# Moving matmul operands to 160 bytes modulo 256 in a two-layer linear-attention and MLP kernel

## The chip, the core and the metric

The kernel runs on one core of a Trainium2 chip. The core has a matmul engine (TensorE, PE in the profile; its weight loads are listed apart as PEld), a vector engine (VectorE, DVE), a scalar engine for activations (ScalarE, ACT), a general engine (GpSimd, POOL) and an engine that here only issues transfers (SyncE, SP). They work on an on-chip memory of 128 partitions; matmul results land in PSUM, in banks of 512 floats a partition. A matmul reads two operands from on-chip memory: the stationary one, which a weight load puts into the array beforehand, and the moving one, which is then streamed through it. "128x448 moving" means 128 partitions by 448 columns.

The metric is the device time of one launch in microseconds (us). Addresses in this document are byte offsets within a partition; a float takes 4 bytes.

## The reference

Input `x` has 2048 tokens of 448 features. Two identical layers follow each other:

```python
def _A_ref(x, wqkv, wo):                       # linear attention, 16 heads of 28
    q, k, v = split(x @ wqkv)
    phi = lambda t: where(t > 0, t + 1, exp(t)) + 1e-6
    pq, pk = phi(q), phi(k)
    kv = einsum("bhsd,bhse->bhde", pk, v)
    z = einsum("bhsd->bhd", pk)
    num = einsum("bhqd,bhde->bhqe", pq, kv)
    den = einsum("bhqd,bhd->bhq", pq, z)[..., None] + 1e-6
    return merge_heads(num / den) @ wo
def _B_ref(x, w1, b1, w2, b2):                 # MLP, 448 -> 1792 -> 448
    return gelu(x @ w1 + b1) @ w2 + b2

x = x + _A_ref(_layernorm(x), wqkv, wo)
x = x + _B_ref(_layernorm(x), w1, b1, w2, b2)  # and both once more
```

## The kernel before

Every large product is computed from split operands. A float32 value `a` becomes `hi` (rounded to the matmul's reduced format, float32r in the code) and `lo = a - hi`, and a product takes three matmuls: hi by hi, hi by lo, lo by hi. A contraction over 448 features is cut into three chunks of 128 and one of 64. The last 64 hold hi and lo stacked in one 128-row operand, so they take two matmuls. One product of 128 tokens therefore takes 3 x 3 + 2 = 11 matmuls.

A layer runs in these stages.

1. `phase1` goes over 16 tiles of 128 tokens. Per tile: normalized tokens are transposed and split into blocks `XH` and `XL`. `proj` (lines 328 to 333) multiplies them, as stationary operands, by the moving pieces of wk or wq (`wkq`), into `psk` and `psq`. `phi` is applied; the keys are split into `kh` (`stage_kh`, line 464) and `kl`. The untransposed normalized tokens are split into `xnh` and `xnl` (`stage_s`). `stage_g` (lines 526 to 541) accumulates G = tokens-transposed by keys: stationary `xnh` or `xnl`, moving `kh` or `kl`. A projection and a G group alternate on TensorE. The queries of some tiles are projected only later, as filling between the steps of stage 2. Queries go to memory as `pq_d`.
2. A transition turns G into one matrix per group of heads with wo folded in, M, split into `Mh` and `Ml` (`trans_ms`). M is copied by transfers into the places of wq, in chunks of 128 rows (`trans_chunks`), since wq is not needed any more.
3. The attention output of four tiles at a time: `o_mm` (lines 792 to 794, first block, moving `Mh`, `Ml`) or `oc_mm` (lines 803 to 807, later blocks, moving the chunks in wq's places), with stationary `qh` and `ql`.
4. The MLP, in four blocks of 512 tokens by 14 slices of 128 hidden features: `mlp1` (lines 861 to 865) has the weights stationary and 512 tokens moving, `hp`. Gelu gives `gh` and `gl`. `mlp2` (lines 894 to 896) has these stationary and `w2h`, `w2l` moving, 448 columns, `y`. The attention output of the next block (`oc_mm`) is worked in between slices after a plan (`PLAN_0`, `PLAN_1`, `PLAN`).

The order of instructions on every engine is written out by hand (`ORDER`, `STEPS`, `LAUNCH`, the plans), and nothing is rescheduled. Engines meet only at semaphores. Transfers are issued on SP's queue in the same written order.

Where tiles lie matters here. Tiles are named by tags; a tag has a fixed number of buffers, placed one behind another where the tag is first used. `t448` makes tiles of 448 floats, 1792 bytes, which is 7 x 256. `t512` makes tiles of 512 floats, or of 576 floats for tags B and F, of which a slice of 512 from column `at` is used. Both sizes are multiples of 256 bytes, and two small tiles named `space` fill up so that the operands of matmuls start on multiples of 256. Three kinds of tile are set off from that by `APART = 28` floats, 112 bytes: `xnl` and `gl` and `ql` of `q_split` (tag B), and `ql` of `q_part` (tag F). These are the lo parts that serve as stationary operands in G, in the second MLP product and in the attention output. All other operands of these matmuls lie at 0 modulo 256.

The pieces of wk have tags W0, W1, W2 (hi of chunks 0 to 2), W3, W4, W5 (lo) and W6 (the stacked last chunk); those of wq have V0 to V6 likewise (`piece`, line 132). W0 to W3 later hold loaded queries (`load_pq`), W4 and W5 products of them, W6 the masked G product `kvm`. V0 to V2 and V6 later hold M's hi chunks and its stacked chunk, V3 to V5 the lo chunks.

Of the kernel before, what the change touches and what calls it, by code (L numbers as in the profile page):

```python
# [9 lines left out]
F32 = mybir.dt.float32  # L10
F32R = mybir.dt.float32r
# [11 lines left out]
def linear_attn_mlp_kernel(  # L23
# [15 lines left out]
    S, D = x0.shape  # L39
    F = w1.shape[1]  # L40
# [4 lines left out]
    G = 112  # L45
# [6 lines left out]
    work = ctx.enter_context(tc.tile_pool(name="work", bufs=2))  # L52
# [14 lines left out]
    def t448(tag, bufs, name, dt=F32):  # L67
        bufs = NH if tag == "H" else bufs
        return work.tile([128, D], dt, name=name, tag=tag, bufs=bufs)

    APART = 28

    def t512(tag, bufs, name, dt=F32, at=0):
        n = 576 if tag in "BF" else 512
        return work.tile([128, n], dt, name=name, tag=tag, bufs=bufs)[:, at:at + 512]

    def f(ap):
        return ap.bitcast(F32)
# [53 lines left out]
    def piece(name, i):  # L132
        return t448(f"{'W' if name == 'k' else 'V'}{i}", 1, f"w{name}{i}", F32R)

    def split_hi(name, c, st):
        hi = piece(name, c if c < 3 else 6)
        act.copy(hi, st[c])
        wkq[name, c] = (hi, piece(name, 3 + c)) if c < 3 else hi
# [22 lines left out]

    ones = consts.tile([128, 128], F32R, name="ones")
    one = t512("e", 3, "one")[:, :128]
    dve.memset(one, 1.0)
    dve.tensor_copy(ones, one)
# [39 lines left out]
    def ln_bn(xs):  # L205
        st = work.tile([128, 6], F32, name="bst", tag="bst", bufs=3)
        dve.bn_stats(st, xs)
        return st
# [11 lines left out]
    def ln_norm(stats, name):  # L220
        xs, mv, rs = stats
        xn = t512("xn", 2, name)
        dve.tensor_scalar(xn[:, :D], xs, mv[:, 0:1], rs, op0=OP.subtract, op1=OP.mult)
        return xn
# [88 lines left out]
    def split_t(key, t, hi, lo, eng=dve):  # L313

        x = spreads[key, t // 2].rearrange("p (i c u n) -> p u c i n", i=4, c=4, n=32)[:, t % 2]
        h = hi.rearrange("p (c i n) -> p c i n", c=4, n=32)
        act.copy(h, x)  # L317
        eng.tensor_tensor(lo.rearrange("p (c i n) -> p c i n", c=4, n=32), x, f(h), op=OP.subtract)  # L318
# [17 lines left out]
    def phi(o, name, into=None, tag="e"):  # L336

        e = t512(tag, 3 if tag == "e" else 2, name)[:, :D]
        act.activation(e, o, AF.Relu, scale=-1.0)
        act.activation(e, e, AF.Exp, scale=-1.0)  # L340
        into = e if into is None else into
        dve.scalar_tensor_tensor(into, o, 0.0, e, op0=OP.max, op1=OP.add)
        return into
# [62 lines left out]
    def stage_a(l, t):  # L406
        sts[l, t] = ln_stats(xt.pop((l, t)))
# [35 lines left out]
    def stage_s(l, t):  # L443
        xn = xns.pop((l, t))
        h = t512("A", 2, "xnh", F32R)
        lo = t512("B", 2, "xnl", F32R, APART)
        act.copy(h[:, :D], xn)  # L447
        pool.tensor_tensor(lo[:, :TL], xn[:, :TL], f(h[:, :TL]), op=OP.subtract)  # L448
        pool.tensor_tensor(h[:, D:], xn[:, TL:], f(h[:, TL:D]), op=OP.subtract)
        split[l, t] = (h, lo)  # L450
# [10 lines left out]
    ke = {}  # L461

    def stage_kh(l, t):
        kh = t512("E", 2, "kh", F32R)[:, :D]
        act.activation(kh, ke[l, t], AF.Identity, bias=tiny)
        ks[l, t] = (kh,)

# [122 lines left out]
    def launch(za):  # L590
        for tok in LAUNCH.split():
            name, (j, *c) = tok.rstrip("0123456789"), [int(i) for i in tok if i.isdigit()]
            if name in ("ka", "qa"):
                split_hi(name[0], j, st_k if name == "ka" else st_q)
            elif name in ("kb", "qb"):
                split_lo(name[0], j, st_k if name == "kb" else st_q, pool if tok in ("kb1", "kb2", "qb0", "qb2") else dve)
            elif name in ("ha", "hb", "la", "lb"):
                split_half(("a", 0, 0), j, "ab".index(name[1]), "hi" if name[0] == "h" else "lo")
            elif name == "T":
                launch_t(j)  # L600
            elif name == "K":
                stage_k(0, j, c)
            elif name == "Q":
                stage_q(0, j, c)
            elif name == "kl":
                stage_kl(0, j, za)
            else:
                {"a": stage_a, "n": stage_n, "kp": stage_kphi, "kh": stage_kh, "s": stage_s}[name](0, j)

    def phase1(l, tr):  # L610
# [6 lines left out]
        for t in range(l == 0, NT):  # L617
            norm = NORM[l][t] if t < len(NORM[l]) else ()
            for tok in STEPS.get((l, t), STEP).split():
# [16 lines left out]
                elif tok == "tu":  # L636
                    for u in norm:
                        stage_t(l, u)
                elif tok == "D":
                    pe.transpose(bank("h", 2, "turn")[:, :128], ident, ident)  # L640
                elif tok == "T" and t + 1 < NT:
                    stage_b(l, t + 1, "acc" if t == 1 else "h")
                elif tok == "X" and t + 1 < NT and (l == 0 or t + 1 >= 4):
                    stage_x(l, t + 1)
                elif tok == "K":
                    stage_k(l, t)
                elif tok == "qp":
                    stage_qphi()
                elif tok == "kp":
                    stage_kphi(l, t)  # L650
                elif tok == "kh":
                    stage_kh(l, t)
                elif tok == "kl":
                    stage_kl(l, t, za)
                elif tok == "s":
                    stage_s(l, t)
                elif tok == "G" and t >= 1:
                    acc = acc or [bank("acc", 4, f"G{c}")[:, :D] for c in range(4)]
                    stage_g(l, t - 1, acc)
                elif tok == "bg" and l == 0:  # L660
                    background(BG[t], 1 if t >= 8 else 2)
                elif tok == "Q" and t < DEFER:
                    stage_q(l, t)
# [50 lines left out]
    def trans_ms(tr, g):  # L714
        if g == 0:
            tr.Mh, tr.Ml = [], []
        if g % 2 == 0:
            for n in ("Mh", "Ml")[:1 if g else 2]:
                s = work.tile([128, 1024], F32R, name=n, tag="S", bufs=5)
                getattr(tr, n).extend(s[:G, i * D:(i + 1) * D] for i in range(2))  # L720
        if g >= 2:
            tr.Ml.append(t512("F", 2, "Ml", F32R)[:G, :D])
        act.copy(tr.Mh[g], tr.mp[g])
        dve.tensor_sub(tr.Ml[g], tr.mp[g], f(tr.Mh[g]))
# [20 lines left out]
    pqt, qs, pzs = {}, {}, {}  # L745
# [31 lines left out]
    def q_split(l, b, j):  # L777
        tp = tqs.pop((l, b, j))
        qh = t512("A", 2, "qh", F32R)[:G]
        ql = t512("B", 2, "ql", F32R, APART)[:G]  # L780
        act.copy(qh, tp[:G])
        dve.tensor_sub(ql, tp[:G], f(qh))
        qs[l, b, j] = (qh, ql)
# [55 lines left out]
        turn(pqt.pop((l, b * 4 + j)), ("q", l, b), j)  # L839

    def q_part(l, b, j):
        qs[l, b, j] = t512("E", 2, "qh", F32R), t512("F", 2, "ql", F32R, APART)
        split_t(("q", l, b), j, *qs[l, b, j])

    def m_prep(l, b, j):
# [9 lines left out]
    def mlp1(l, b, i):  # L855
# [12 lines left out]
        gh = t512("A", 2, "gh", F32R)  # L868
        gl = t512("B", 2, "gl", F32R, APART)
        act.copy(gh, g)  # L870
# [115 lines left out]
    table(AF.Exp)  # L986
    stage_a(0, 0)
    work.tile([128, 32], F32, name="space", tag="space", bufs=1)
    bn = ln_bn(xt[0, 1])
    split_hi("k", 0, st_k)  # L990
    stage_n(0, 0)
# [4 lines left out]
    for l in range(LAYERS):  # L996
        tr = SimpleNamespace(mp={})
# [10 lines left out]
        def pre(j):  # L1008
# [8 lines left out]
            ld=lambda j: (load_pq(l, 0, j), load_x(l, j)), z=lambda j: trans_z(tr, zs[l]), gt=lambda j: trans_gt(tr, acc),  # L1017
            kv=lambda j: trans_kv(tr), mask=lambda j: trans_mask(tr), m=lambda j: trans_m(tr, j),
            ms=lambda j: trans_ms(tr, j), qz=lambda j: q_z(l, 0, j, tr), qs=lambda j: q_scale(l, 0, j, tr),
            tq=lambda j: q_transpose(l, 0, j), qq=lambda j: q_split(l, 0, j), o=lambda j: o_mm(l, 0, j, tr),  # L1020
            la=lambda j: o_ln(l, 0, j), lb=lambda j: o_n(l, 0, j), T=lambda j: m_transpose(l, 0, j),
            x=lambda j: m_split(l, 0, j), tu=lambda j: turn(xns.pop(("m", l, j)), ("m", l, 0), j),
            st=lambda j: store_sq(("m", l, 0), 0), sp=lambda j: spread(("m", l, 0), 0), pre=pre, b=biases)
        for tok in ORDER.split():
            name, j = tok.rstrip("0123456789"), int("0" + tok.lstrip("abcdefghijklmnopqrstuvwxyzQTG"))
# [69 lines left out]
```

## Time and profile before

| | us |
|---|---|
| runs of the kernel before | 870.06, 871.63, 871.71 |
| their median | 871.63 |
| the profiled execution | 870.69 |
| its span, first to last instruction | 869.0 |
| TensorE busy | 863.5 |
| VectorE busy | 491.6 |
| ScalarE busy | 344.7 |
| GpSimd busy | 221.5 |

The profiled execution is one run; its span leaves out 1.7 us around the first and the last instruction. The page gives busy time by engine, slices of the span, and the chain of work that ended last: from the last instruction back, at each step, to what released it. In the chain, each matmul stands with the time until the next one starts, so the chain's rows give the pace of TensorE. In lists of instructions a matmul's duration reaches beyond the start of the next one, since matmuls are pipelined and their ends are modelled; these durations overlap and do not add up to the span.

### The profile page before, as it was taken

To read this page: it belongs to the slowest core of one execution; us is meant where nothing else is said; L and a number is where in the kernel's file an instruction comes from. 1 tells how busy PE (TensorE), PEld (TensorE's weight loads), DVE (VectorE), ACT (ScalarE), POOL (GpSimd) and SP (SyncE) were. 2 spreads that over 40 slices of the span, in tenths; PEclk is the share of its full clock that TensorE was granted. 3 is DMA by queue.
4 is the path that set the end of the run, shared out by engine and by line. 5 is a ranking of instruction groups with operands and counts; after the bars stand their busy time and mean duration, and the time that the engine had idled before them with its cause. 6 is when DMAs were issued, how large, how long until landed. Compare 5 with 4: busy or idle time off the path is not lost.

```text
span 869.0 us, 11679 instructions
## 1 busy us (share of the span) xinstructions
PE 863.5 (99%) x4182; PEld 771.0 (89%) x4182; DVE 491.6 (57%) x958; ACT 344.7 (40%) x606; POOL 221.5 (25%) x250
## 2 busy tenths in 40 slices
PE   9999999999999999999999999999999999999998
PEld 8999888888888888888899998888888888888887
DVE  6888496658456443226477876864674483533112
ACT  6776635324323322333355665342233133223231
POOL 5566532235012102012222344120220140140000
PEclk9999999999999999999999999999999999999999
DMA  5474736624313402051145443252332413111001
GB/s 160 139 234 158 210 89 205 193 89 131 134 60 105 158 0 98 1 181 49 49 145 184 165 133 106 98 182 90 105 115 92 129 68 125 49 49 42 1 1 43
DMA packets 63642, 94.76 MB, mean 109 GB/s; under 512 B 8928, under 2 KB 58720, under 8 KB 63584
## 3 DMA queue, kind: packets, MB, share of 16 engines
q1 hardware_dynamic: 63408, 93.87, 33.6%
q8 instruction: 33, 0.54, 0.3%
q14 instruction: 25, 0.20, 0.1%
q10 hardware_dynamic: 176, 0.14, 0.0%
HBM read 56.17 MB, written 34.60 MB: 104 GB/s over the span
## 4 chain that ended last, share of the span: by engine, by line
PE 98%; DMA 0%; DVE 0%; ACT 0%; POOL 0%; issue 0%; SPq 0%; DVEq 0%; ACTq 0%
PE y L895 10%; PE y L894 10%; PE y L896 10%; PE hp L863 9%; PE hp L861 9%; PE hp L862 9%; PE hp L865 3%; PE hp L864 3%; PE psk L329 2%; PE psq L329 2%; PE psq L328 2%; PE psq L330 2%; PE psk L330 2%; PE psk L328 2%; PE G L538 2%; PE G L537 2%
## 5 line engine op out<-in xcount | busy, mean ns | idle before, releaser
L871 DVE TENSOR_TENSOR gl<-g,gh 128x512 fp32r<-128x512 f32 x112 | 83.2, 743 | 294.4 <-ACT gh L870 294.4
L867 ACT ACTIVATE g<-hp,b1s 128x512 f32<-128x512 f32 x112 | 77.1, 688 | 400.9 <-PE hp L865 392.6
L895 PE MATMUL y<-w2l,gh 128*128 128x448 f32 x447 | 163.6, 366 | 0.0
L894 PE MATMUL y<-w2h,gh 128*128 128x448 f32 x447 | 162.0, 362 | 0.0
L896 PE MATMUL y<-w2h,gl 128*128 128x448 f32 x447 | 160.0, 358 | 0.0
L863 PE MATMUL hp<-XL,w1h 128*128 128x512 f32 x336 | 130.9, 390 | 0.0
L862 PE MATMUL hp<-XH,w1l 128*128 128x512 f32 x336 | 130.7, 389 | 0.0
L861 PE MATMUL hp<-XH,w1h 128*128 128x512 f32 x336 | 130.7, 389 | 0.0
L217 POOL TENSOR_TENSOR brs<-bve,mhalf 128x1 f32<-128x1 f32 x64 | 39.4, 616 | 281.0 <-DVE bve L215 277.9
L894 PEld LDWEIGHTS y<-w2h,gh 128*128 128x128 f32 x447 | 83.7, 187 | 9.4
L895 PEld LDWEIGHTS y<-w2l,gh 128*128 128x128 f32 x447 | 83.9, 188 | 7.0
L896 PEld LDWEIGHTS y<-w2h,gl 128*128 128x128 f32 x447 | 84.0, 188 | 5.0
L863 PEld LDWEIGHTS hp<-XL,w1h 128*128 128x128 f32 x336 | 63.1, 188 | 13.6 <-issue 0.6
L861 PEld LDWEIGHTS hp<-XH,w1h 128*128 128x128 f32 x336 | 63.0, 187 | 10.6
L862 PEld LDWEIGHTS hp<-XH,w1l 128*128 128x128 f32 x336 | 63.1, 188 | 9.9
L870 ACT CAST gh<-g 128x512 fp32r<-128x512 f32 x112 | 69.6, 622 | 3.6
L754 POOL TENSOR_TENSOR pz<-pq,zb 128x448 f32<-128x448 f32 x32 | 36.7, 1148 | 81.9 <-DVE dn L760 61.0
L448 POOL TENSOR_TENSOR xnl<-x,xnh 128x384 fp32r<-128x384 f32 x32 | 35.2, 1099 | 72.1 <-ACT xnh L447 40.1
L318 DVE TENSOR_TENSOR XL<-sp,XH 128x512 fp32r<-128x512 f32 x50 | 44.6, 898 | 4.3 <-ACT XH L317 4.3
L865 PE MATMUL hp<-XL,w1x 128*128 128x512 f32 x112 | 43.6, 389 | 0.0
L864 PE MATMUL hp<-XH,w1x 128*128 128x512 f32 x112 | 43.6, 389 | 0.0
L823 POOL TENSOR_TENSOR x<-x,b2b 128x448 f32<-128x448 f32 x32 | 41.9, 1331 | 0.0
(169 smaller groups left out, 1565.2 us busy)
## 6 DMA issues: line engine op xcount, KB each, us to landing
x<-in_A_x_dram SPq DMA_DIRECT2D x32, 224.0 KB, 4.0
pq_d<-eq SPq DMA_DIRECT2D x32, 224.0 KB, 2.7
pq<-pq_d SPq DMA_DIRECT2D x32, 224.0 KB, 3.3
sq_m<-sq SPq DMA_DIRECT2D x14, 512.0 KB, 2.8
sp<-sq_m SPq DMA_DIRECT2D x56, 128.0 KB, 2.8
x<-x_d SPq DMA_DIRECT2D x32, 224.0 KB, 3.4
sq_a<-sq SPq DMA_DIRECT2D x12, 512.0 KB, 2.9
sp<-sq_a SPq DMA_DIRECT2D x48, 128.0 KB, 3.1
```

Of the source, the lines that this page charges most:

```text
L318: eng.tensor_tensor(lo.rearrange("p (c i n) -> p c i n", c=4, n=32), x, f(h), op=OP.subtract)
L861: pe.matmul(o, w1h[:, c, s], x.moving(x.hi, c), start=(c == 0), stop=False)
L862: pe.matmul(o, w1l[:, c, s], x.moving(x.hi, c), start=False, stop=False)
L863: pe.matmul(o, w1h[:, c, s], x.moving(x.lo, c), start=False, stop=False)
L864: pe.matmul(o, w1x[:, s], x.moving(x.hi, 3), start=False, stop=False)
L865: pe.matmul(o, w1x[:, s], x.moving(x.lo, 3), start=False, stop=True)
L867: act.activation(g, hp, AF.Gelu_apprx_tanh, bias=b1s[:, i:i + 1])
L870: act.copy(gh, g)
L871: dve.tensor_sub(gl, g, f(gh))
L894: pe.matmul(acc[j], gh[:, s], w2h[:, i], start=first, stop=False)
L895: pe.matmul(acc[j], gh[:, s], w2l[:, i], start=False, stop=False)
L896: pe.matmul(acc[j], gl[:, s], w2h[:, i], start=False, stop=stop)
```

## The change

Only addresses change. Four edits:

- A second constant, `BEHIND = 40` floats, 160 bytes. At the start, before the first use of their tags, the eight tiles W0, W1, W2, W6, V0, V1, V2 and V6 are allocated in one row behind a filler of 160 bytes, and a filler of 96 bytes follows. So the hi pieces and the stacked pieces of wk and wq lie at 160 modulo 256, and whatever uses these places later does too. The lo pieces W3 to W5 and V3 to V5 stay at 0.
- `kh` (tag E) and `Mh` (tag S) start 40 floats into their tiles, at 160 modulo 256.
- `xnl`, and `ql` in both of its places, go from 112 back to 0.
- Tag F is no longer 576 floats wide but 512, since nothing in it is set off any more. `gl` keeps its 112.

```diff
-    APART = 28
+    APART, BEHIND = 28, 40
     def t512(tag, bufs, name, dt=F32, at=0):
-        n = 576 if tag in "BF" else 512
+        n = 576 if tag == "B" else 512
...
     def stage_s(l, t):
-        lo = t512("B", 2, "xnl", F32R, APART)
+        lo = t512("B", 2, "xnl", F32R)
...
     def stage_kh(l, t):
-        kh = t512("E", 2, "kh", F32R)[:, :D]
+        kh = t512("E", 2, "kh", F32R)[:, BEHIND:][:, :D]
...
             for n in ("Mh", "Ml")[:1 if g else 2]:
                 s = work.tile([128, 1024], F32R, name=n, tag="S", bufs=5)
-                getattr(tr, n).extend(s[:G, i * D:(i + 1) * D] for i in range(2))
+                at = BEHIND if n == "Mh" else 0
+                getattr(tr, n).extend(s[:G, at + i * D:][:, :D] for i in range(2))
...
     def q_split(l, b, j):
-        ql = t512("B", 2, "ql", F32R, APART)[:G]
+        ql = t512("B", 2, "ql", F32R)[:G]
...
     def q_part(l, b, j):
-        qs[l, b, j] = t512("E", 2, "qh", F32R), t512("F", 2, "ql", F32R, APART)
+        qs[l, b, j] = t512("E", 2, "qh", F32R), t512("F", 2, "ql", F32R)
...
     work.tile([128, 32], F32, name="space", tag="space", bufs=1)
+    work.tile([128, BEHIND], F32, name="ahead", tag="ahead", bufs=1)
+    for name in "kq":
+        for i in (0, 1, 2, 6):
+            piece(name, i)
+    work.tile([128, 64 - BEHIND], F32, name="behind", tag="behind", bufs=1)
```

## The prediction

> **What bounds the kernel now.** I read the page first, then the waits of TensorE, then single lines, then the chain that ended last in short windows.
>
> ```profile
> span 869.0 us, 11679 instructions
> PE 863.5 (99%) x4182; PEld 771.0 (89%) x4182; DVE 491.6 (57%) x958; ACT 344.7 (40%) x606; POOL 221.5 (25%) x250
> PEclk9999999999999999999999999999999999999999
> PE 98%; DMA 0%; DVE 0%; ACT 0%; POOL 0%; issue 0%; SPq 0%; DVEq 0%; ACTq 0%
> ```
> ```profile
> PE warm L170 <- DVE one L164: 1.1, 1, 1.1
> PE tp L267 <- ACT b2b L416: 0.4, 1, 0.4
> PE tp L267 <- DVE x L412: 0.3, 1, 0.3
> ```
>
> TensorE is busy 99% of the span, 98% of the chain runs over it, its granted clock never drops, and in 869 us it waits 1.8 us for other engines. So the time is the sum of the distances from one matmul's start to the next one's. An edit that moves only addresses can change the time only through these distances, or by making some other engine or a transfer late enough to stop TensorE.
>
> A duration in the list of instructions is no distance, since matmuls overlap, but it follows it (rows of single lines, minimum/median/maximum in ns):
>
> ```profile
> L329 PEld LDWEIGHTS psk<-wk,XH x96: 186/188/191, 7.4 to 524.3; 128*128 128x128 f32 x96
> L329 PE MATMUL psk<-wk,XH x96: 358/365/476, 7.5 to 524.5; 128*128 128x448 f32 x96
> L894 PE MATMUL y<-w2h,gh x447: 362/362/368, 142.8 to 864.0; 128*128 128x448 f32 x149
> L895 PE MATMUL y<-w2l,gh x447: 365/366/366, 143.0 to 864.2; 128*128 128x448 f32 x149
> L896 PE MATMUL y<-w2h,gl x447: 358/358/358, 143.2 to 864.4; 128*128 128x448 f32 x149
> ```
>
> All four matmuls have the same shape, 128x128 stationary and 128x448 moving, yet they last 358 to 366 ns, and each line of the second MLP product keeps its value 447 times almost without spread. That is no waiting for data; it is something fixed for each pair of operands. The weight load of 186 to 191 ns nearly fills a distance of 200 ns, so a few ns around the load show in the next start. The distances themselves come from the chain (start in us, length, engine, tile, line):
>
> ```profile
> 579.53 0.20 PE y L894
> ...
> 581.93 0.23 PE hp L861
> ...
> 584.43 0.20 PE y L894
> ```
> ```profile
> 60.46 0.20 PE psq L328
> ...
> 62.69 0.20 PE psk L328
> ...
> 64.92 0.20 PE G L537
> ```
>
> First fence: twelve matmuls of the second MLP product (L894 to L896, four times) in 581.93 - 579.53 = 2.40 us, 200 ns each; then eleven 512-wide ones in 2.50 us, 227 each. Second fence: one projection of q and one of k, eleven matmuls each, in 4.46 us: **202.7 ns each** for the same 448 columns. The program says what differs. In the MLP product the lo part of the stationary operand (gl) lies 112 bytes past a multiple of 256, and hi part and weights lie on one. In the projections all four operands lie on multiples of 256. Two places between these:
>
> ```profile
> 64.92 0.20 PE G L537
> ...
> 67.14 0.20 PE psq L328
> ```
> ```profile
> 98.70 0.20 PE G L537
> ...
> 100.94 0.20 PE psq L328
> ```
> ```profile
> 594.21 0.20 PE op L803
> ...
> 596.42 0.21 PE y L894
> ```
> ```profile
> 133.46 0.21 PE psq L328
> ...
> 134.91 0.20 PE psq L333
> ```
>
> G (L537 to L541, lo at 112) takes 2.22 or 2.24 us for eleven, 201.8 to 203.6 each: behind an all-zero projection it needs some matmuls to come down to 200, and in some tiles it never does. The attention output (L803 to L807, lo at 112) takes 2.21 us for eleven, 200.9 each. And the same all-zero projection can also run worse: behind a group of transposes seven of them take 1.45 us, 207.1 each. So this shape has a best pace of 200 and a bad one of about 207; 202.7 is three matmuls at the best pace to two at the bad one. No group in these rows goes below 200, and I take that as the floor.
>
> **The change part by part.** No instruction is added, removed or reordered; the eight early allocations only fix addresses and are never written. Nothing new waits, and no queue changes. What moves:
>
> (a) wk and wq, hi pieces (W0, W1, W2, W6, V0, V1, V2, V6), moving operand of L328, L330, L332, L333: from 0 to 160 modulo 256. The lo pieces stay at 0, XH and XL at 0. These are 2 layers x 16 tiles x 2 projections x 11 = 704 matmuls. At the floor they save 2.7 x 704 = 1.90 us.
>
> (b) kh to 160 and xnl back from 112 to 0, in G: 2 x 16 x 11 = 352 matmuls, now around 202.5. At the floor: 2.5 x 352 = 0.88 us.
>
> (c) Mh to 160 (L792 to L794, 2 x 4 x 12 = 96 matmuls), the V pieces that later hold Mh's chunks to 160 (L803 to L807, 2 x 12 x 11 = 264), ql back to 0 in both. Now 200.9: at the floor 0.9 x 360 = 0.32 us.
>
> So 1416 matmuls (704 + 352 + 360) get one new pattern: stationary at 0 throughout, moving 160, 0, 160 by turns. The trace shows it nowhere: no moving operand of this shape lies off a multiple of 256, only stationary ones. Its price per matmul is bounded by the nearest rows: 200.0 below and 207.1 above. I take 200, because the one staggered pattern that the trace does show, lo at 112, runs at 200 in 447 x 3 matmuls, and the new one too sets the two operands apart by no multiple of 256: by 96 (0 - 160 modulo 256) in two matmuls of three, where the old one had 112 in one of three. That is nearest in kind, not a proof, and both ends stay in the range. At the floor the sum is 1.90 + 0.88 + 0.32 = 3.1 us. Some is lost where a tile starts behind transposes or a pause and the pace has to settle; I take five sixths, **2.6 us**.
>
> The Trainium skill, "TensorE: Matmul & The Clock Gate", section "Step-by-step: what each phase is for", speaks against all this: it says that TensorE reads the moving operand and the weight load through two independent ports, and that loading the next weights does not steal bandwidth from the running matmul. By that the sum would be 0. The rows above disagree in part, since equal shapes run at 200 and 202.7; they can't say that the addresses do it.
>
> (d) Everything else that touches the moved tiles: ACT and DVE write kh and the hi pieces, DMA fills W0 to W2 with pq and V with M's chunks. I cost these at nothing, with this cover:
>
> ```profile
> 16.00:97.00 81.00, 80.96 (x411) 74.30 (x410) 66.05 (x134) 56.35 (x110) 47.34 (x58) 1.00 0.53 167
> L465 ACT ACTIVATE kh<-psk,tiny x32: 626/636/637, 14.6 to 527.4; 128x448 fp32r<-128x448 f32 x32
> DMA to landing us min/median/max: 2.6/3.3/5.1
> ```
>
> In the first row (busy time of PE, weight loads, DVE, ACT, POOL in the k and q stage) DVE has 66 of 81 us. A stage 1.3% shorter makes that 83%, so DVE still follows. Were each of the 32 kh writes 10% slower, that is 2.0 us on ACT, which has 25 us free in that window alone. A pq load lands in 3.3 us, 5.1 at worst, and no wait of TensorE for a DMA stands in the list; a load slower by half would still be POOL's wait first. If the cover went, a late kh would hold the G group one tile on, at most a few tenths of a us a tile. I keep 0 for (d).
>
> **Sum.** The profiled execution took 870.69 us (span 869.0 and 1.7 around it): 870.69 - 2.6 = 868.1. The median of the runs, 871.63, lies 0.94 above it; from there 871.63 - 2.6 = **869.0 us**. A measurement of this kernel can tell about 0.2%, 1.74 us, from no change. One ns over all 1416 matmuls is 1.42 us and they now average about 202.2, so the verdict is faster below a new average of 201.0 and slower above 203.4.
>
> **The rivals.**
> Slower: the new pattern falls into the bad pace. For it speaks that the all-zero projection does so itself behind transposes (207.1), that G with lo at 112 doesn't always reach 200 (203.6), and that moving operands off a multiple of 256 are new in two matmuls of three. Against it speaks the steady 200 of the only staggered pattern shown. If two of three are bad, the average is (200 + 2 x 206.7) / 3 = 204.5 and the time (204.5 - 202.2) x 1.416 = +3.3 us, 874.9; if all are, +6.4 us, 878.0. It decides from 203.4 on.
>
> No use: the new pattern does what all-zero does, 202.7. The projections stay, G pays 0.2 x 352 = 0.1 and the output 1.8 x 360 = 0.6 us, since they give up the lo at 112: +0.7 us, 872.3, below what can be told. Its variant is that addresses don't set the pace at all, and the 2.7 ns come from the stage (other engines reading and writing at the same time): 871.6. For that speaks that the projections run while DVE and ACT are at their busiest; against it, that G and the projections alternate in the same stage at different paces. The page named above would give this variant.
>
> Half of it: the projections reach 200, G and the output stay as they are: -1.9 x 5/6 = -1.6 us, 870.0.
>
> **How the numbers follow.** Floor reached: 0.47, 869.0 (867.2 to 870.0: the lowest of the runs shown, 870.06, less 2.9, up to the half case). Half of it: 0.10. No use, both variants: 0.13. Bad pace: 0.30. Faster by over 0.2%: 0.47 and a third of the half case, 0.50. Within: 0.13 and the rest of the half case, 0.20. Slower: 0.30. The range goes up to the case of two bad in three, 874.9, and leaves out all bad at one end: 867.2 to 874.9.
>
> **What would show it.** Right: 22 matmuls of a pair of projections in 4.40 us instead of 4.46, eleven of G in 2.20, eleven of the output in 2.20, the median of L329 near 362, the second MLP product unchanged at 2.40 for twelve. Wrong: projections at 4.5 or more, or the output above 2.21, which (c) alone can cause. If waits of TensorE rise well above 1.8 us, (d) failed.

## The result and the profile after

The changed kernel is slower: median 872.41 us against 870.52 us before, ratio 1.0021 with a 95% interval of 1.0012 to 1.0029. The measured time lies inside the stated range, but the change went the other way: the forecast took 2.6 us off a median of 871.63 us from three runs, and against the median of all thirteen, 1.9 us were added. The profiled execution took 872.35 us, 1.66 us more than the one before.

The page of the changed kernel, and its list of what TensorE waited for:

```profile
span 870.6 us, 11679 instructions
PE 864.7 (99%) x4182; PEld 770.7 (89%) x4182; DVE 492.5 (57%) x958; ACT 344.5 (40%) x606; POOL 221.5 (25%) x250
```
```profile
PE warm L170 <- DVE one L164: 1.1, 1, 1.1
PE tp L267 <- DVE x L412: 0.6, 1, 0.6
PE tp L267 <- ACT b2b L416: 0.5, 1, 0.5
```

The same instructions, the other engines as busy as before, and 2.2 us of waits instead of 1.8, at the very start. So most of the loss lies in the distances between matmuls, as the chain shows (start in us, length, engine, tile, line; behind line 719 the numbers are one higher than before):

```profile
60.82 0.20 PE psq L328
...
65.30 0.20 PE G L537
...
67.54 0.20 PE psq L328
```
```profile
595.56 0.20 PE op L804
...
597.80 0.20 PE y L895
...
600.00 0.20 PE y L897
```

The 22 matmuls of a pair of projections take 4.48 us (4.46 before, 4.40 forecast), eleven of G 2.24 (2.22 or 2.24 before, 2.20 forecast), eleven of the output 2.24 (2.21 before, 2.20 forecast). The second MLP product behind them is unharmed: eleven in 2.20 us.

The table shows the rest. It is worked out from the starts of all matmuls in the two traces. The pace is the mean distance from one start to the next, leaving out distances above 215 ns (above 245 ns in the first MLP product), which hold a wait or a switch to or from transposes; the total is the sum of all distances.

| product | matmuls | pace before, ns | pace after, ns | total before, us | total after, us |
|---|---|---|---|---|---|
| k projection | 352 | 202.7 | 203.6 | 72.42 | 72.51 |
| q projection | 352 | 202.8 | 203.7 | 71.93 | 72.19 |
| G | 352 | 202.4 | 203.6 | 71.95 | 72.26 |
| output, first block | 96 | 201.0 | 203.8 | 19.65 | 19.91 |
| output, later blocks | 264 | 200.6 | 203.7 | 52.96 | 53.78 |
| first MLP product | 1232 | 226.7 | 226.7 | 279.64 | 279.67 |
| second MLP product | 1341 | 200.1 | 200.0 | 268.36 | 268.18 |

The totals rise by 1.59 us, almost the whole 1.66 by which the profiled executions differ; 1.08 of them are in the output, which gave up its pattern with lo at 112. The k projection pays less than its pace says: before, one near 92 us lost about 0.25 us to late token splits behind a transfer and to the keys that G waited for, and after, TensorE comes later and doesn't wait there.

One place in the changed kernel's own trace points to the cause. In one tile of each layer G's matmuls are ordered differently: four and three with kh moving (lines 529, 531), then four with kl (line 533):

```profile
94.42 0.82 PE G L529 x4
95.24 0.60 PE G L531 x3
95.84 0.81 PE G L533 x4
96.65 0.21 PE psk L328
```

The moving operand stays at 160 for seven matmuls, and the last three of them take 0.60 us, 200 ns each; the four behind them, at 0, take 0.81 us, 202.5 each. The pattern 160, 0, 160 runs at 203.6.

### The profile page after: what moved, and what is told of

Same layout as the page of the kernel before. It is cut to its first block, busy times and chain, and to the rows that moved or that the text cites. A ratio compares the mean times of both kernels' runs of the same rounds, so it can differ in the third digit from the quotient of the medians.

```text
span 870.6 us, 11679 instructions
## 1 busy us (share of the span) xinstructions
PE 864.7 (99%) x4182; PEld 770.7 (89%) x4182; DVE 492.5 (57%) x958; ACT 344.5 (40%) x606; POOL 221.5 (25%) x250
## 4 chain that ended last, share of the span: by engine, by line
PE 98%; DMA 1%; DVE 0%; ACT 0%; POOL 0%; issue 0%; SPq 0%; DVEq 0%; ACTq 0%
PE y L896 10%; PE y L895 10%; PE y L897 10%; PE hp L864 9%; PE hp L862 9%; PE hp L863 9%; PE hp L866 3%; PE hp L865 3%; PE psk L329 2%; PE psq L330 2%; PE psq L329 2%; PE psq L328 2%; PE psk L330 2%; PE psk L328 2%; PE G L539 2%; PE G L537 2%
```

## The experiments

The question was what in the new pattern costs. The offset of an address modulo 256 is called its place. The *distance* is the place of the next weight load's operand minus the place of the operand that is then streaming, modulo 256. The theories, by their letters in the expectations: **A**, the distance counts and must stay constant and other than 0. **B**, a moving operand off a multiple of 256 costs by itself. **C**, only the lo at 112 ever helped. **D**, each change of the moving operand's place costs. **E**, only the distance counts and its changes are free.

Paces of all runs (ns, worked out as above), each from one trace. Products whose addresses are the same modulo 256 differ a little between the runs: all-zero ones run at 202.7 to 203.1, and G of the kernel before went from 202.4 to 201.8 and 201.5 when only the tokens' lo moved. Differences of a few tenths of a ns are therefore not read as effects of a product's own addresses.

| kernel | k proj. | q proj. | G | first output | later outputs | ratio to before |
|---|---|---|---|---|---|---|
| before | 202.7 | 202.8 | 202.4 | 201.0 | 200.6 | 1 |
| changed | 203.6 | 203.7 | 203.6 | 203.8 | 203.7 | 1.0021 (1.0012 to 1.0029) |
| all moving 160 | 200.9 | 201.4 | 200.8 | 201.1 | 202.8 | 1.0005 (0.9997 to 1.0014) |
| q part undone | 203.8 | 203.0 | 203.5 | 200.7 | 200.6 | 1.0005 (0.9996 to 1.0014) |
| token lo 96 | 203.2 | 203.0 | 201.8 | 202.4 | 200.7 | 1.0067 (1.0054 to 1.0081) |
| four constant offsets | 200.7 | 203.4 | 203.7 | 203.9 | 203.5 | one run, 870.89 us |
| tokens at 96 | 205.1 | 204.4 | 202.5 | 202.3 | 202.0 | 1.0140 (1.0123 to 1.0157) |
| k both 160 | 203.0 | 205.3 | 205.4 | 202.2 | 202.7 | one run, 885.05 us |
| lo moving off | 203.2 | 203.2 | 203.3 | 204.7 | 203.6 | one run, 871.91 us |
| token lo 64 | 202.8 | 203.3 | 201.5 | 201.3 | 201.5 | one run, 877.31 us |
| changes alone | 203.3 | 203.4 | 203.6 | 204.2 | 202.5 | one run, 871.99 us |
| all moving 64 | 200.2 | 200.3 | 200.2 | 200.6 | 200.7 | 0.9978 (0.9969 to 0.9987) |
| k and G at 160 | 201.8 | 203.1 | 200.7 | 200.6 | 200.6 | 1.0004 (0.9995 to 1.0013) |

### All moving operands at 160

```diff
-        for i in (0, 1, 2, 6):
+        for i in range(7):
             piece(name, i)
...
-        kl = t512("F", 2, "kl", F32R)[:, :D]
+        kl = t512("F", 2, "kl", F32R)[:, BEHIND:][:, :D]
...
-                at = BEHIND if n == "Mh" else 0
+                at = BEHIND
...
-            tr.Ml.append(t512("F", 2, "Ml", F32R)[:G, :D])
+            tr.Ml.append(t512("F", 2, "Ml", F32R)[:G, BEHIND:][:, :D])
```

> The changed kernel, but with every moving operand of the k, q, G and output products at 160 modulo 256, the lo ones too (W0 to W6, V0 to V6, kh, kl, Mh, Ml); stationary operands at 0. Theory A: what costs is that the distance between the weight load's address and the running stream's changes from matmul to matmul (160, 0, 160); with one constant distance other than 0 all 1416 matmuls run at 200.0 ns, projections 4.40 us for 22, G and output 2.20 us for 11, about 3 us faster than before and 5 faster than the changed kernel. Theory B: a moving operand off a multiple of 256 costs by itself; now three of three are off, the average goes above the 203.7 ns of the changed kernel to 205 or more, 3 to 6 us slower than before. Theory C: only lo at 112 helps and the place of the moving operand does nothing; all groups as the all-zero projection before, 202.7 ns, 0.8 us slower than before.

In the chain, a k projection of the second layer and one of the first, from its first to its eleventh matmul:

```profile
451.05 0.20 PE psk L328
...
453.05 0.20 PE psk L333
```
```profile
41.55 0.20 PE psk L328
...
43.62 0.20 PE psk L333
```

Ten distances in 2.00 us, a flat 200, and the same ten in 2.07 us, a flat 207. With the lo operands beside the hi ones the projections and G reach the floor in most tiles; so 160 alone is no harm, and B falls for this shape; so does C, since no lo of these products lies at 112. But the same addresses also hold a steady slow pace. The slow tile shown is the third in a row: the pace came up in the G group right behind four transposes and held through a q and a k projection. Other G groups behind the same transposes settle at 200, so the transposes alone don't decide it. The later outputs, which start behind 512-wide matmuls at place 0, need six slow matmuls to settle and average 202.8.

The whole kernel did not get faster: the interval of the ratio includes no change. Part of the gain turned into waits in the first layer. In the chain:

```profile
86.96 3.44 DMA sp<-sq_a
90.40 0.02 issue
90.42 0.04 ACTq L317
90.46 0.04 issue
90.50 0.63 ACT XH L317
91.13 0.02 issue
91.15 0.70 DVE XL L318
91.86 0.04 issue
91.90 0.47 PE psk L330
```

TensorE now arrives before this transfer and its two splits. Distances above 215 ns grew by 1.0 us in the k projection, 1.3 in the first output and 0.7 in the first MLP product, and the slow starts cost the later outputs another 0.6.

### The q part undone

```diff
-    for name in "kq":
-        for i in (0, 1, 2, 6):
-            piece(name, i)
+    for i in (0, 1, 2, 6):
+        piece("k", i)
...
-                at = BEHIND if n == "Mh" else 0
+                at = 0
...
-        ql = t512("B", 2, "ql", F32R)[:G]
+        ql = t512("B", 2, "ql", F32R, APART)[:G]
...
-        qs[l, b, j] = t512("E", 2, "qh", F32R), t512("F", 2, "ql", F32R)
+        qs[l, b, j] = t512("E", 2, "qh", F32R), t512("F", 2, "ql", F32R, APART)
```

(Tag F is 576 floats wide again, and the filler of 160 bytes holds a small tile to save room.)

> The changed kernel with its output and q part undone: V pieces and Mh at 0, ql back at 112; wk's hi pieces and kh at 160, xnl at 0 stay. From the paces of the changed kernel (projection 203.7, G 203.6 against 202.7 and 202.4): k projection +0.3 us and G +0.4 us, q projection 202.7 and output 200.7 ns as before. So 0.7 to 0.8 us slower than before, and 1.1 us or more faster than the changed kernel. If the loss came from DMA or from the engines that touch the shifted W and V tiles, the output's pace would stay bad or TensorE's waits would rise.

```profile
594.27 0.20 PE op L804
...
596.47 0.21 PE y L895
```

The output is back at 2.20 us for eleven. Median 871.01 us, 0.64 above the 870.37 of the runs of before taken with it, where 0.7 to 0.8 were expected; the interval includes no change. k and G keep their bad pace. The paces fit a loss made up product by product. Nothing points to transfers or other engines: TensorE's waits for other engines did not rise (1.1 us).

### The tokens' lo at 96

```diff
             self.hi = work.tile([128, 2048], F32R, name="XH", tag="XH", bufs=2)
+            if not blocks:
+                work.tile([128, 24], F32, name="apart", tag="apart", bufs=1)
             self.lo = work.tile([128, 2048], F32R, name="XL", tag="XL", bufs=2)
```

(on the kernel before; fillers behind it bring the next tiles back to 0)

> The kernel before with one difference: the block of transposed lo tokens (XL), stationary in the projections, starts at 96 modulo 256; all moving operands at 0. The projections then have the pattern that G, output and second MLP product have before (stationary 0, 0, 96; moving 0), near the distance of 160 (0 - 160 is 96 modulo 256). Theory C and the reading of the prediction (a staggered lo runs at the floor): projections at 200 to 201.8 ns, 0.6 to 1.9 us faster than before. Theory A in its pure form, any change of distance costs: projections no better than 202.7. In the first MLP product XL is moving; if that counts there, its 227 ns go up.

The projections got no better, 203.2 and 203.0, though their pattern is now G's old one with 96 for 112. So a stationary lo set off by 96 is no recipe by itself, and the likeness of 96 and 112 that the prediction leaned on fails; 112 itself was not tried in the projections. The main effect was elsewhere. In the first MLP product this block is the moving operand; eleven of its matmuls:

```profile
172.14 0.23 PE hp L866
...
174.68 0.20 PE op L808
```

2.54 us instead of 2.49 or 2.50, 230.9 instead of 226.7 ns on average. Over 1232 matmuls that is 5.1 us, nearly all of the 5.3 us lost.

### Four constant places

```diff
+    at_k, at_q = 16, 32            # floats: wk at 64, wq at 128
...
-        kh = t512("E", 2, "kh", F32R)[:, BEHIND:][:, :D]
+        kh = t512("E", 2, "kh", F32R)[:, 56:][:, :D]      # kl likewise: 224
...
-                at = BEHIND
+                at = 8                                    # Mh and Ml at 32
```

(on the kernel with all moving operands at 160)

> All moving operands at one offset per product, stationary at 0: wk 64, wq and M's chunks 128, kh and kl 224, Mh and Ml 32. Theory A: 200.0 ns in each group where the offset is far enough from 0; 32 and 224 may show how near is too near. Theory B: groups worse than 202.7, most where the offset is no multiple of 64. Theory C: 202.7 everywhere.

The k projection (64, up to the next G) and the q projection (128, from its first line to its last):

```profile
63.03 0.20 PE psk L328
...
64.62 0.20 PE G L537
```
```profile
100.90 0.20 PE psq L328
...
102.33 0.21 PE psq L333
```

Eight distances in 1.59 us, 199, and seven in 1.43, 204. Constant is not enough; the distance matters: with the moving operand at 64 (distance 192) it runs at 200.7, at 128 (distance 128) at 203.4, at 224 (distance 32) at 203.7, at 32 (distance 224) at 203.9. Each distance stands on one product here, apart from 128 (203.4 and 203.5). Since 64 and 128 are both multiples of 64, B's guess about such multiples is wrong too.

### Both token blocks at 96

```diff
+            if first:
+                work.tile([128, 24], F32, name="ahead", tag="ahead", bufs=1)
             self.hi = work.tile([128, 2048], F32R, name="XH", tag="XH", bufs=2)
             self.lo = work.tile([128, 2048], F32R, name="XL", tag="XL", bufs=2)
...
-        lo = t512("B", 2, "xnl", F32R, APART)
+        lo = t512("B", 2, "xnl", F32R)
...
-        kh = t512("E", 2, "kh", F32R)[:, :D]
+        kh = t512("E", 2, "kh", F32R)[:, 40:][:, :D]      # kl likewise
```

> The kernel before with both blocks of transposed tokens (XH and XL, stationary in the projections) at 96 modulo 256, kh and kl both at 160, xnl at 0; wk, wq, M, qh, ql and the second MLP product as before. No moving operand changes its offset from one matmul to the next within a product. Theory A (the distance from the running stream to the next load counts, and a constant 96 runs at 200.0): projections and G at 200.0 to 200.9 ns, as in the run with all moving operands at 160, though here it is the stationary operand that moves; output as before (200.7), first MLP product 227 as before. 2.7 us come free, of which the run with all moving at 160 saw about half eaten by waits for transfers and VectorE in the first layer: 0.8 to 2 us faster than before. If instead the moving operand's own address counts, projections stay at 202.7 and the time at that of before.

A k and a q projection in its chain:

```profile
63.53 0.21 PE psk L334
...
65.18 0.20 PE G L543
```
```profile
112.36 0.20 PE psq L336
...
114.16 0.44 PE tq L778 x4
```

Eight in 1.65 us, the flat 206.7, and nine in 1.80, the flat 200. These are the two paces of the run with all moving operands at 160, which has the same distance of 96 made the other way round. Here most k projections fell into the slow one. The kernel came out 12.3 us slower, where 0.8 to 2 us less were expected. Of the 12.3 us by which the total of all products grew, 9.4 are in the first MLP product again (289.0 instead of 279.6), whose moving blocks now both lie at 96; the second MLP product has 1.4, and the projections and later outputs the rest:

```profile
187.33 0.23 PE hp L867
...
189.68 0.23 PE hp L871
```

Ten distances in 2.35 us, 235 ns. Its moving operand is four separate blocks of 512 bytes. There the moving place 96 does cost, also without any change from one matmul to the next, as B says. But the weights lie at 0 throughout, so the place and the distance are not told apart for this shape.

### k with both operands at 160

```diff
-    at_k, at_q = 16, 32
+    at_k, at_q = 40, 0             # wk at 160, wq at 0; XH and XL at 160
...
+        kh, kl: 24 floats (96); Mh, Ml: 48 floats (192)
```

(on the kernel with four constant places, with 160 bytes ahead of XH)

> Distances worked through with no changes of the moving operand's offset inside a product: k projection stationary 160 and moving 160 (distance 0), q projection stationary 160 and moving 0 (160), G stationary 0 and moving 96 (160), first block's output moving 192 (64), later outputs all 0; first MLP product with both token blocks moving at 160. Theory A: the k projection falls back to the 202.7 of the all-zero pattern, since only the distance counts; q projection and G agree with each other; the later outputs go to 202.7; the first MLP product keeps 227. If the moving address counts by itself, the k projection runs at 200.9 as with all moving at 160.

```profile
63.33 0.20 PE psk L333
...
64.95 0.20 PE G L542
```

Eight in 1.62 us, 202.5; the distances repeat the all-zero sequence of the kernel before (203, 202, 203, 199, 207 ns) although both operands lie at 160. And a stationary 160 under a moving 0 (q projection, 205.3) equals a stationary 0 under a moving 96 (G, 205.4): the same distance of 160. So where the places stay constant, the distance orders the 448-wide products better than either place does; the distance of 96 agrees less well (200.8 to 201.4 against 204.4 and 205.1), since it has two paces. Of the 14.9 us by which the totals of all products grew, the first MLP product with both moving blocks at 160 has 8.7, G, q and the later outputs 2.3 together, and the second MLP product 4.0, though its own addresses are those of before. Two of its groups of twelve, each up to the next hp:

```profile
192.11 0.20 PE y L900
...
194.53 0.23 PE hp L867
```
```profile
197.10 0.20 PE y L900
...
199.55 0.24 PE hp L867
```

They take 2.42 and 2.45 us, against 2.40 before. In the trace, 66 of 108 such groups end at 200 ns, most of them after a slow start, and 42 keep 204.4 to their last matmul. So the pattern with lo at 112, on which the prediction rested, has a second steady pace too. Its own places didn't move, so something that ran before it must bring that about.

### Only the lo moving operands set off

```diff
     for name in "kq":
         for i in (0, 1, 2, 6):
             piece(name, i)
+    for name in "kq":
+        work.tile([128, 16], F32, name=f"ahead{name}", tag=f"ahead{name}", bufs=1)
+        for i in (3, 4, 5):
+            piece(name, i)                                  # 64 for wk, 128 for wq
...
-        kl = t512("F", 2, "kl", F32R)[:, :D]
+        kl = t512("F", 2, "kl", F32R)[:, 8:][:, :D]         # 32; Ml at 96
```

(on the changed kernel, with kh and Mh back at 0 and no other fillers ahead)

> Stationary operands all at 0, hi moving at 0, lo moving off by another amount in each product: wk lo 64, wq lo (and M's lo chunks) 128, kl 32, Ml 96. Two changes of the moving offset in three matmuls, as in the changed kernel. Theory D: each change of the moving operand's offset costs about 6.7 ns (six changes in eleven matmuls are 40 ns: 203.6 ns). If that holds for any change, all groups are at 203.6 or more; if it counts modulo 64 only, the k projection (64) and the q projection and later outputs (128) stay at the all-zero 202.7 or better and G (32) and the first output (96) are at 203.6 or more.

All five products lie between 203.2 and 204.7, whichever the amount: none comes near the floor, and all are above the 202.7 to 203.1 of all-zero products, though in the projections and G by a few tenths only. Neither 64 nor 128 escapes.

### The tokens' lo at 64

The same edit as with 96, with 16 floats instead of 24.

> The kernel before with XL at 64 instead of 0 (it was 96 in an earlier run): stationary in the projections, moving in the first MLP product, where the weight load leaves some 36 ns of slack, so that only changes of the moving offset can show. With 96 that product went from 226.7 to 230.9 ns. Theory D for any change: again about 231 ns, 5 us slower than before. Theory D modulo 64: 227 ns, and the time within 1 us of before.

877.31 us: the first MLP product took 5.7 us more than before, 0.6 of it in one longer wait. Its pace is 230.9 ns, the same as with 96. So there a change by 64 costs as one by 96 did.

### The change alone

```diff
+    for i in (3, 4, 5):  piece("k", i)       # wk lo at 64
+    for i in (0, 1, 2, 6):  piece("q", i)    # wq hi at 64
...
+    for i in (0, 1, 2, 6):  piece("k", i)    # wk hi at 160
+    for i in (3, 4, 5):  piece("q", i)       # wq lo at 160
...
-        h = t512("A", 2, "xnh", F32R)
+        h = t512("A", 2, "xnh", F32R, BEHIND)
```

(on the changed kernel)

> Tells apart what costs in the pattern 160, 0, 160: the change of the moving operand's offset, or the matmuls in between whose distance is another. G: kh 160, kl 0, xnh 160, xnl 0, so the moving offset changes as in the changed kernel, but the distance from the running stream to the next load is 0 throughout. k projection: hi moving at 160 and lo at 64, q projection and later outputs: hi 64 and lo 160, stationary 0, so the distance goes 96, 192, 96 (or 192, 96, 192), both of which run near 200 when constant; Mh 160, Ml 0 as in the changed kernel. Theory D (the change costs, some 6.7 ns each): G, k and q at 203.6 or more. Theory E (only the distance counts, and its changes cost nothing): G 202.7 with the all-zero pattern, k and q near 200.7.

```profile
72.47 0.20 PE G L537
...
74.10 0.20 PE psk L328
```

G takes 1.63 us for eight and 203.6 ns on average, exactly as in the changed kernel, though its distance is 0 throughout, which runs at 202.7 to 203.1 where the places stay. k and q run at 203.3 and 203.4, though each of their two distances runs at 200.2 to 201.4 when it is constant. So E falls: a moving place that changes from matmul to matmul loses the floor, even between two good distances. That it is the place and not the distance whose change counts rests on G alone, by 0.5 to 0.9 ns, and G's stationary place changes here too; this is not settled. D's price of 6.7 ns a change was worked out from the changed kernel (six changes in eleven matmuls, 40 ns of 2240), which is no test of it, and it doesn't hold everywhere: the later outputs came to 202.5 with the same six changes.

### All moving operands at 64

The kernel with all moving operands at 160, with 16 floats in the place of 40.

> All moving operands of the k, q, G and output products at 64 modulo 256, stationary at 0; a constant 64 ran at 200.7 ns in the k projection of the run with four offsets, reached after one or two matmuls. Theory A: k, q and G 200.7, outputs 201 to 202 (they start behind 512-wide matmuls at offset 0); against before -0.7, -0.7, -0.6 us and about +0.1, less 0.5 to 1 us of waits in the first layer: 0.5 to 1.3 us faster than before, 871.6 to 870 where the run before would be 870.4 to 871, and 2.5 to 3 us faster than the changed kernel.

```profile
60.31 0.20 PE psq L328
...
66.31 0.20 PE psq L328
```

Thirty matmuls in 6.00 us: projections and G at the floor of 200. Median 868.73 against 870.50 us, ratio 0.9978 (0.9969 to 0.9987): this version is faster than the kernel before, by 1.8 us, and its median lies some 3.7 below that of the changed one, which was measured apart. The gain is above the 0.5 to 1.3 us expected, as the paces came out at 200.2 and not 200.7. Of the 2.8 us that the prediction gave the projections and G at the floor, 2.6 are there (k 1.05, q 0.79, G 0.78 us in the totals), less 0.3 us in the first output and 0.8 in the first MLP product, where TensorE now waits for VectorE:

```profile
135.61 1.36 DVE XL L318
136.97 0.61 DVE XL L273
137.59 0.14 issue
137.72 0.47 PE hp L864
```

### k and G at 160

All seven W pieces, kh and kl at 160 and xnl at 0, on the kernel before; q and output untouched.

> The kernel before with all of wk's pieces and kh, kl at 160 and xnl at 0; q projection and outputs as before (moving 0, ql 112). Theory A: k projection 200.9 and G 200.8 ns (where all moving operands at 160 had them), q 202.8, outputs 200.6 to 201; -0.6 and -0.5 us, less 0.5 us for a wait at the end of the first layer's tiles: 0 to 1 us faster than before. The q projections between could leave the k projection in its slow pace of 206.7, which a constant distance of 96 also showed; then it is no faster.

G came as expected (200.7) and k 0.9 ns slower (201.8, with some tiles settling only after six matmuls). The profiled execution, 869.54 us, is the fastest of its eleven runs. The runs did not show a gain: ratio 1.0004 (0.9995 to 1.0013). That is inconclusive, as 1 us is about what it can tell.

## Why the prediction was wrong

**What bounds the kernel.** Right. The time is the sum of the matmuls' distances, 200 ns, averaged over a few matmuls, is the floor of the 448-wide shape in every run, and about 207 the slowest steady pace seen.

**The price of the new pattern, parts (a) to (c).** This step failed: "I take 200, because the one staggered pattern that the trace does show, lo at 112, runs at 200 ... and the new one too sets the two operands apart by no multiple of 256". Being apart is not what brings 200. In these runs a product reached 200 only with the moving place held constant, and with the stationary operand either at one good distance from it or in the old pattern with lo at 112; the new pattern changes the moving place in two of three steps. It measured 203.6 to 203.8 in all five products, where 200 was taken, so that the terms came to +0.35 us in (a), +0.31 in (b) and +1.08 in (c), where -1.90, -0.88 and -0.32 stood. Held against the runs, the analogy fails in both directions: a constant distance of 96 reached 200 (all moving at 160), the alternating 160, 0, 160 did not, and a stationary lo at 96 in the projections gave 203. The prediction's own rows held a warning: the same lo at 112 ran at 201.8 to 203.6 in G. Why alternating costs, inside the engine, stays open.

**The sum.** Adding up the distances was right and was fed the wrong pace: 1416 matmuls now average 203.66 ns against 202.14 before, and 1.52 ns x 1.416 is 2.2 us; the medians are 1.9 apart. The bound given there for a slower verdict, 203.4, was just passed. The start of the sum, a median of three runs, was 1.1 us too high, which brought the forecast time nearer to the result by luck.

**The rival "slower".** Its sign came true, at 0.30 where the floor had 0.47, and narrowly: the interval of the ratio, 1.0012 to 1.0029, has the 0.2% inside. Its mechanism is not shown: with two matmuls in three at the bad pace of 206.7 the average would be 204.5 and the loss 3.3 us, while the single distances in the trace lie spread out, nearly all from 200 to 207, and average 203.7. Nor is the all-zero 202.7 a mix of a best and a bad pace, as the prediction read it: its single distances go in a sequence such as 203, 202, 203, 199, 207. The sign that the prediction named for the output, above 2.21 us, came at 2.24; the one for the projections, 4.5, was not reached at 4.48, though they were not at 4.40 either. The median of L329 stayed at 365 and did not go to 362.

**"No use" and "half of it".** Both fail as mechanisms, though the time of the first, 872.3, is as near as can be to what was measured; that is luck. The projections did not stay at 202.7 and did not reach 200, G and the output lost more than the return to all-zero would cost, and the place of the moving operand does count. The Trainium skill says in "TensorE: Matmul & The Clock Gate", "Step-by-step: what each phase is for", that a weight load doesn't steal from the running matmul. By that alone the addresses would not matter here, and these runs don't fit it: with equal instructions the pace moved between 200.2 and 205.4 ns as the distance between the two operands changed. Which of the two reads is held up is not shown.

**Part (d), everything else at nothing.** Right as far as the runs show: the waits of TensorE rose from 1.8 to 2.2 us, all at the start. The cover matters in the other direction: when the matmuls do get faster, the first layer's splits and transfers take back part of it, as in the run with all moving operands at 160.

## What to carry to other kernels

When TensorE is the bound and equal matmuls show different distances, look at the addresses of both operands before the schedule: keep the moving operand's place modulo 256 the same from one matmul to the next, and then try a few constant places against the stationary operand, because some run at the floor and some don't; here 64 against a stationary 0 was the best. Measure each on its own product in one run, since the trace gives the pace product by product, and a whole-kernel time of two parts in a thousand does not. Don't extend a pattern that works in one product to another by likeness: the product before it is part of what sets the pace, as the second MLP product showed, and an operand that two products share has to suit both: the token blocks, moved for the projections, cost the first MLP product 5 to 9 us.

## What the runs showed that I had not expected

- A constant distance of 96 has two steady paces with the same addresses, 200 and 206.7 ns, held for whole tiles. How the engine comes into the one or the other was not found out, nor why the pattern with a stationary lo at 112 runs at 200 although its distance changes.
- The paces by constant distance have no plain order. Distance 0: 202.7 to 203.1 ns, 203.0 with both operands at 160; 32: 203.7; 64: 202.2 (first output only); 96: 200 or 206.7 by tile; 128: 203.4 and 203.5; 160: 205.3 and 205.4; 192: 200.2 to 200.7; 224: 203.9 (first output only).
- The 512-wide product with four separate blocks has the opposite taste: place 0 gives 226.7 ns, both moving blocks at 96 or at 160 give 234.3 and 233.9, which costs 9.4 and 8.7 us over its 1232 matmuls.
- That 256 bytes is the right unit in which to count places was taken over from the kernel before; no run tests it by itself.
